# A second staging buffer for q, a shared one for w_spatial, v's key chunks even before odd, and a new step order in a fused attention and gMLP kernel

## Chip, cores, metric

One core of one Trainium2 chip. The metric is the device time of one execution in microseconds; lower is better. Engines are called TensorE (PE in the profile; PEld is its weight load), VectorE (DVE), ScalarE (ACT), GpSimd (POOL) and SyncE (SP, which issues most DMA loads).

## The reference

Grouped-query attention feeds a gMLP block, 8 batches of 384 rows:

```python
scores = q @ k.T / sqrt(64)            # 16 q heads, 4 kv heads, head_dim 64
attn   = softmax(scores)
x      = (attn @ v) as (8, 384, 1024)  # heads side by side
h      = relu(x @ w_in)                # 1024 x 1024
u, v   = h[..., :512], h[..., 512:]
v_n    = (v - mean(v)) / sqrt(var(v) + 1e-6)
v_s    = w_spatial @ v_n + b_spatial   # over the 384 rows
out    = (u * v_s) @ w_out             # 512 x 1024
```

## The kernel before

All work is a hand-ordered list of steps: one text (FIRST) starts batches 0 to 2, one (STEADY) is run for batches 3 to 6, one (LAST) ends. A step is a letter code with its batch: S a pair of score matmuls, E their exp, X the product with v (part 2 gives the row sums), V the v half of x @ w_in, G a pair of half-array groups, lq/lk/lws loads, cq/ck/cws casts to fp16, Tq/Tk/Tw transposes by TensorE, tq/tk/tw the copies of their results, dq/dk transposes by DMA, W a warm-up matmul without use. Each engine takes its own steps in this order and none ahead of it. The last field of a step names an engine: v VectorE, s ScalarE, p GpSimd.

```python
def new_q32(b, gp):                    # fp32 q of one kv pair, one buffer per pair
    loaded["q32", b, gp] = ld.tile(
        [P, 2 * G, NST * D], FP32, name=f"q32_{b}_{gp}", tag=f"q32_{gp}"
    )

def load_w_out(m):
    w32 = stage.tile([P, DM], FP32, name=f"w32_{m}", tag="w32", bufs=2)
    ...

def load_ws():
    ws32 = stage.tile([P, NST, S], FP32, name="ws32", tag="ws32", bufs=1)
    nc.sync.dma_start(ws32, moe_w_spatial.rearrange("(p tt) s -> p tt s", tt=NST))
    loaded["ws32"] = ws32

def score_mm(b, u, j0=0, js=1):
    sc = ps_sc.tile([P, 2, 512], FP32, ..., tag="sc")   # pool ps_sc has two buffers
    ...

def v_mm(b, st, k0=0, k1=NKT):
    ...
    for kc in range(k0, k1):
        nc.tensor.matmul(held["pv", b, st], xT[b][:, kc, ...], w_in16[:, kc, DH:DFF],
                         start=(kc == 0), stop=(kc == NKT - 1))

def norm(b, st):                       # v_n in fp16 from v_r in fp32, both in SBUF
    nc.vector.tensor_scalar(v_n, held["v_r", b, st], mean, rstd,
                            op0=ALU.subtract, op1=ALU.mult)
```

The softmax here doesn't subtract the row's maximum and nothing guards it: scores larger than these inputs give would overflow.

## Time and profile before

| | |
|---|---|
| median of the first 3 runs | 249.28 us (248.23, 249.28, 249.32) |
| the profiled execution | 247.47 us, of which 245.7 from first to last instruction |
| TensorE busy | 97% |

The profile is of one execution. Note for later that this one is 1.8 us faster than the median. The lines of the profile are shown with the prediction. A line of the timeline is: start, duration, engine, source line, operation, out<-in, form, count, and in brackets how long the engine had been idle and what ended that. A line of the waits is: who waited, for whom, total us, times, longest.

### The profile page before, as it was taken

What the parts mean: (1) busy time and instruction counts of PE and PEld (TensorE: products, weight loads), DVE (VectorE), ACT (ScalarE), POOL (GpSimd) and SP (SyncE); (2) the same over time, 40 slices, a digit from 0 to 9 for tenths busy, and PEclk for the clock granted to TensorE, in tenths of its full rate; (3) what the DMA queues carried; (4) which work ended last, traced back from release to release, by engine and by line L of the source; (5) the groups of instructions that cost most, each with busy time, mean ns of one, the idle gap of its engine ahead of it and who ended that gap; (6) DMA issues with size and microseconds to landing.
All of it is one profiled execution on the core that took longest, in us unless ns stands there. A gap on an engine that the chain in (4) does not pass through costs nothing.

```text
span 245.7 us, 6038 instructions
## 1 busy us (share of the span) xinstructions
PE 238.5 (97%) x2556; PEld 114.8 (47%) x2556; DVE 153.1 (62%) x304; ACT 179.7 (73%) x229; POOL 43.9 (18%) x83
## 2 busy tenths in 40 slices
PE   7899999999999999999999999999999999999993
...
ACT  2899999999997778779697787788697797500111
...
GB/s 180 292 211 329 275 256 183 186 309 238 148 210 312 114 235 147 148 60 279 246 223 3 187 296 141 183 30 258 204 197 13 0 173 85 4 69 16 31 230 254
DMA packets 57756, 42.73 MB, mean 174 GB/s; under 512 B 26881, under 2 KB 53889, under 8 KB 57729
## 3 DMA queue, kind: packets, MB, share of 16 engines
...
q10 hardware_dynamic: 1184, 0.39, 0.6%
...
## 4 chain that ended last, share of the span: by engine, by line
PE 93%; ACT 4%; DMA 1%; issue 0%; DVE 0%; POOL 0%
PE X L395 20%; PE sc L368 13%; PE pu L613 13%; PE po L640 12%; PE pv L600 12%; PE pv L438 5%; PE psp L626 5%; PE po L545 4%; PE pu L510 4%; ACT aT L381 3%; PE psp L484 2%; DMA k<-in_k_dram 1%; PE pq L349 1%; PE sc_u L510 1%; PE po L574 0%
## 5 line engine op out<-in xcount | busy, mean ns | idle before, releaser
L381 ACT ACTIVATE aT<-sc 128x1024 f16<-128x1024 f32 x144 | 139.5, 1023 | 19.7 <-PE sc L368 19.5
L640 PE MATMUL po<-w_out,gT 64*128 64x512 f16 x288 | 66.4, 376 | 0.0
L600 PE MATMUL pv<-w_in,xt 64*128 64x512 f16 x272 | 64.2, 376 | 0.0
L368 PE MATMUL sc<-qT,kT 64*128 64x512 f16 x288 | 49.5, 378 | 1.4 <-ACT aT L381 1.3
L424 DVE TENSOR_TENSOR xt<-X,rec 128x512 f16<-128x512 f32 x48 | 31.7, 684 | 15.8 <-ACT aT L381 6.4
L328 DVE COPY osb<-po 128x512 f32<-128x512 f32 x41 | 28.1, 689 | 14.1 <-PE po L640 8.6
L395 PE MATMUL X<-aT,v 128*32 128x512 f16 x576 | 35.9, 380 | 0.0
L613 PE MATMUL pu<-xt,w_in 64*128 64x384 f16 x384 | 35.2, 323 | 0.0
L640 PEld LDWEIGHTS <-gT 64*128 64x128 f16 x288 | 25.6, 94 | 16.1 <-DVE mark_v L694 3.1
L600 PEld LDWEIGHTS <-xt 64*128 64x128 f16 x272 | 25.1, 94 | 15.8 <-issue 2.5
L328 POOL CAST q<-q 128x768 f16<-128x768 f32 (+2 forms) x27 | 20.6, 775 | 53.3 <-DMA q<-in_q_dram 43.3
L522 DVE SCALAR_TENSOR_TENSOR gT<-pu,v_s 128x384 f16<-128x384 f32 x31 | 16.0, 553 | 18.6 <-PE pu L613 15.9
L368 PEld LDWEIGHTS <-kT 64*128 64x128 f16 x288 | 15.1, 94 | 23.5 <-issue 11.9
L613 PEld LDWEIGHTS <-w_in 64*128 64x128 f16 x384 | 18.4, 94 | 14.9 <-issue 1.7
L496 DVE TENSOR_TENSOR v_s<-psp,bias_b 128x384 f32<-128x384 f32 x32 | 20.4, 687 | 3.8 <-PE psp L626 3.0
L395 PEld LDWEIGHTS <-v 128*32 128x32 f16 x576 | 14.8, 97 | 16.5 <-issue 2.8
L395 PE MATMUL X<-aT,ones 128*32 128x512 f16 x288 | 20.0, 382 | 0.0
L406 ACT ACTIVATE rec<-X 128x512 f32<-128x512 f32 x23 | 13.8, 602 | 8.3 <-PE X L395 8.0
L326 ACT ACTIVATE osb<-po 128x512 f32<-128x512 f32 x6 | 3.6, 598 | 18.6 <-PE po L545 17.6
L459 DVE BATCH_NORM_STATS2 stats<-v_r 128x6 f32<-128x512 f32 x24 | 16.6, 691 | 0.7 <-ACT v_r L451 0.5
L412 ACT ACTIVATE rec<-rec 128x512 f32<-128x512 f32 x23 | 14.5, 630 | 0.6
L470 DVE TENSOR_SCALAR v_n<-v_r,mv,rstd 128x512 f16<-128x512 f32 x24 | 12.3, 539 | 3.9 <-issue 2.7
...
## 6 DMA issues: line engine op xcount, KB each, us to landing
...
```

The costliest lines, as they stand in the source:

```text
L328: engine.tensor_copy(dst, src)
L368: nc.tensor.matmul(sc[:, half, 0 : 512 // js], kT[b][lo:hi, gp, t, :], qT[b, gp][lo:hi, qt, j0::js], start=True, stop=True,)
L381: nc.scalar.activation(aT[b, qt][:, gp, t].rearrange("p h (j q) -> p h j q", j=G)[:, :, j0::js], held["sc", b, u, j0][:, :, 0 : 512 // js] ...
L395: nc.tensor.matmul(dst[32 * g : 32 * (g + 1), :], v16[:, g, t, 32 * part : 32 * (part + 1)] if part < 2 else ones32, a[:, g // 2, t, g % 2 ...
L412: nc.scalar.activation(r, r, AF.Exp, scale=-1.0)
L424: nc.vector.tensor_tensor(xt[:, jj, :, qt * P : (qt + 1) * P], held["X", b, qt, jj].rearrange("p (j q) -> p j q", j=G), held["rec", b, qt] ...
L459: nc.vector.bn_stats(s6, held["v_r", b, st])
L496: nc.vector.tensor_tensor(held["v_s", b][:, m, :].rearrange("p (t s) -> p t s", t=NST), held["psp", b, m][:, 0:S].rearrange("p (t s) -> p ...
L522: nc.vector.scalar_tensor_tensor(held["gT", b][:, mu, :], held["pu", b, mu][:, 0:S], 0.0, held["v_s", b][:, mu, :], op0=ALU.max, op1=ALU.mult,
L600: yield lambda kc=kc: nc.tensor.matmul(held["pv", b, st], xT[b][rows, kc, st * P : (st + 1) * P], w_in16[rows, kc, DH:DFF], start=(first a ...
L613: yield lambda kc=kc: nc.tensor.matmul(held["pu", b, mu][:, 0:S], w_in16[rows, kc, mu * P : (mu + 1) * P], xT[b][rows, kc, :], start=(firs ...
L640: yield lambda m=m: nc.tensor.matmul(held["po", b, i], held["gT", b][rows, m, tt * P : (tt + 1) * P], w_out16[rows, m, half * 512 : (half ...
```

## The change

The intent is to let loads go out earlier and to shorten the start: q of the first kv pair gets a second buffer, paid for by staging w_spatial in w_out's buffers and its fp16 cast in an output buffer; v is contracted with the even key chunks first, as these need only one of the two multiplies that make x; and the steps are put in another order, with some casts and evictions on other engines.

```diff
-            [P, 2 * G, NST * D], FP32, name=f"q32_{b}_{gp}", tag=f"q32_{gp}"
+            [P, 2 * G, NST * D], FP32, name=f"q32_{b}_{gp}", tag=f"q32_{gp}", bufs=2 - gp
...
-        w32 = stage.tile([P, DM], FP32, name=f"w32_{m}", tag="w32", bufs=2)
+        w32 = stage.tile([P, NST * S], FP32, name=f"w32_{m}", tag="w32", bufs=2)[:, :DM]
...
-        ws32 = stage.tile([P, NST, S], FP32, name="ws32", tag="ws32", bufs=1)
+        w32 = stage.tile([P, NST * S], FP32, name="w32_s", tag="w32", bufs=2)
+        ws32 = w32.rearrange("p (t s) -> p t s", t=NST)
...
-            loaded["ws16"] = stage.tile([P, NST, NST, P], FP16, name="ws16", tag="ws16", bufs=1)
+            osb = out_pool.tile([P, DM], FP32, name="osb_ws16", tag="osb")
+            loaded["ws16"] = osb.bitcast(FP16)[:, : NST * S].rearrange(
+                "p (s t q) -> p s t q", s=NST, t=NST
+            )
...
+    KC_ORDER = [*range(0, NKT, 2), *range(1, NKT, 2)]
...
-        for kc in range(k0, k1):
+        for n in range(k0, k1):
+            kc = KC_ORDER[n]
```

The three step lists are new throughout. Cut to the steps named, other steps between them left out:

```diff
 FIRST
-(22 warm-ups) Tk,0,0,0,3 W,0,4 W,0,4 tk,0,0,0,3,v cq,0,0,0,1,1,0,1,v Tq,0,0,0,0,1
+(27 warm-ups) Tk,0,0,0,3 W,0,4 cq,0,0,0,1,1,0,1,v Tq,0,0,0,0,1 ... tk,0,0,0,3,s
-lk,2 lws,0 lq,2,0 lbi,0
+lws,0 lk,2 lq,2,0 lbi,0
-S X,0,2,2 V,0,1,4,8 Tq S S X,0,2,0 X,0,2,1 S
+S X,0,2,2 X,0,2,1 X,0,2,0 S S Tq V,0,1,4,8 Tq S
-ck,2,1,0,3,p cq,1,1,1,3,0,0,1,p cws,0,0 ... cws,0,2 cws,0,1 ck,2,0,0,3,p
+cws,0,0 ... cws,0,1 ... cws,0,2 ... ck,2,1,0,3,v ... ck,2,0,0,3,s
 STEADY
-rl,0,0 re,0,0 E E ru,-1,2,s           (ScalarE's order at the start of a period)
+rl,0,0 E cq,1,1,0,3,1,0,1,s re,0,0 ck,1,0,0,3,s E oc,-2,2,s oc,-2,3,s
```

More of the change, by code (lines that the diff above doesn't have):

```diff
@@ L21 @@
 FIRST = """
-W,0,1 W,0,4 lk,0,0,2 lq,0,0,0,1,0,1,s lq,0,1,0,1 W,0,4 W,0,2 W,0,2 W,0,2 W,0,3 W,0,4 lk,0,2,4
-cq,0,0,0,1,0,0,1,s lq,0,0,1,3 lq,0,1,1,3 lk,1 lv,0 lv,1 lq,1,0 lq,1,1 ck,0,0,0,3,p Tk,0,0,0,3 W,0,4
-W,0,4 tk,0,0,0,3,v cq,0,0,0,1,1,0,1,v Tq,0,0,0,0,1 tq,0,0,0,0,1,v W,0,4 ck,0,1,0,3,p
-cq,0,1,0,1,1,0,1,p cq,0,1,0,1,0,0,1,p S,0 lk,2 E,0 lws,0 S,0 Tk,0,1,0,3 W,0,4 W,0,2 lq,2,0 lbi,0
-Tq,0,1,0,0,1 S,0 lwi,0,1,1 lwi,0,1,2 lwi,0,1,3 cq,0,0,1,3,0,0,1,p tq,0,1,0,0,1,v tk,0,1,0,3,v
-cq,0,1,1,3,1,0,1,p cq,0,0,1,3,1,0,1,v W,0,2 E,0 W,0,1 S,0 lq,2,1 E,0 S,0 Tq,0,0,1,0,1 W,0,1 W,0,2
@@ L28 @@
-S,0 cq,0,1,1,3,0,0,1,v tq,0,0,1,0,1,v Tq,0,1,1,0,1 S,0 W,0,4 ck,1,1,0,3,p ck,1,0,0,3,p lwi,0,1,0
-cv,0,p S,0 W,0,1 Tq,0,1,2,0,1 Tk,1,0,0,3 tk,1,0,0,3,v tq,0,1,1,0,1,v tq,0,1,2,0,1,v Tq,0,0,2,0,1
-tq,0,0,2,0,1,v E,0 E,0 E,0 E,0 E,0 S,0 X,0,0,2 S,0 S,0 X,0,0,0 E,0 S,0 rv,0,0 X,0,0,1 xm,0,0,0 E,0
-E,0 S,0 E,0 X,0,1,2 E,0 S,0 xm,0,0,1 X,0,1,1 X,0,1,0 S,0 rl,0,1 E,0 re,0,1 cq,1,0,0,1,0,0,1,p E,0
-S,0 Tk,1,1,0,3 V,0,0,0,4 V,0,0,4,8 lwi,0,0,3 S,0 S,0 cq,1,1,1,3,1,0,1,p lwi,0,0,0 lwi,0,0,2 cv,1,v
-xm,0,1,1 xm,0,1,0 E,0 ck,2,1,0,3,p cq,1,1,1,3,0,0,1,p cws,0,0 lwi,0,0,1 cq,1,0,1,3,1,0,1,v cws,0,2
@@ L34 @@
-cws,0,1 ck,2,0,0,3,p cq,1,0,0,1,1,0,1,s tk,1,1,0,3,v E,0 Tq,1,0,0,0,1 V,0,1,0,4 tq,1,0,0,0,1,v
-ru,0,0,v cq,1,0,1,3,0,0,1,v cq,1,1,0,1,0,0,1,v E,0 cq,1,1,0,1,1,0,1,v S,0 X,0,2,2 V,0,1,4,8
-Tq,1,1,0,0,1 ru,0,1,v S,0 tq,1,1,0,0,1,v E,0 rl,0,2 S,0 X,0,2,0 re,0,2 E,0 E,0 X,0,2,1 xm,0,2,0
-xm,0,2,1 S,0 E,0 Tq,1,0,1,0,1 Tq,1,1,1,0,1 V,0,2,0,4 S,0 S,0 cq,2,0,0,3,1,0,1,p cq,2,0,0,3,0,0,1,p
-cq,2,1,0,3,1,0,1,p cq,2,1,0,3,0,0,1,p E,0 E,0 Tw,0,0,2 bs,0,0 tq,1,0,1,0,1,v bs,0,1 tw,0,0,2
-tq,1,1,1,0,1,v Tq,1,0,2,0,1 V,0,2,4,8 X,1,0,2 S,0 S,0 ru,0,2,s X,1,0,0 rl,1,0 tq,1,0,2,0,1,v bs,0,2
@@ L40 @@
-X,1,0,1 lwo,0,1 dk,2 dq,2,0 lwo,0,0 Tw,0,2,3 Tq,1,1,2,0,1 re,1,0 xm,1,0,0 xm,1,0,1 S,0 E,0 rs,0
-V,1,0,0,4 E,0 tq,1,1,2,0,1,v E,0 nm,0,0 V,1,0,4,8 dq,2,1 tw,0,2,3 nm,0,1 S,0 lwo,0,3 nm,0,2 ru,1,0,v
-G,0,gs,2,0,0,1 S,0 lwo,0,2 mk,0,gs,2,v G,0,gs,0,0,0,1 G,0,gs,2,1,0,1 S,0 mk,0,gs,0,v E,0 E,0 E,0
-sa,0,2 G,0,gs,0,1,0,1 S,0 sa,0,1 sa,0,0 sa,0,3 bs,1,0 X,1,1,2 E,0 cwo,0,1,1,p rl,1,1 X,1,1,0 X,1,1,1
-S,0 cwo,0,0,0,p G,0,gu,2,0,0 S,0 re,1,1 xm,1,1,1 xm,1,1,0 G,0,gu,2,0,1 S,0 cwo,0,0,1,p G,0,gu,0,0,0
@@ L45 @@
-E,0 S,0 G,0,gu,0,0,1 mk,0,gu,2,v G,0,gu,2,1,0 lv,2 cwo,0,1,0,v S,0 lq,3,1 lk,3 lq,3,0 mk,0,gu,0,v
-E,0 E,0 E,0 G,0,gu,2,1,1 S,0 G,0,gu,0,1,0 S,0 G,0,gu,0,1,1 E,0 S,0 cwo,0,3,1,p cwo,0,2,0,p gt,0,2
-gt,0,0 gt,0,1 gt,0,3 cwo,0,3,0,v E,0 cwo,0,2,1,v X,1,2,2 X,1,2,1 S,0 S,0 E,0 E,0 rl,1,2 V,1,1,0,4
-re,1,2 E,0 E,0 V,1,1,4,8 S,0 G,0,go,0,0,0 G,0,go,0,0,1 S,0 xm,1,2,1 ru,1,1,v cv,2,p mk,0,go,0,p
-X,1,2,0 bs,1,1 xm,1,2,0 E,0 E,0 S,0 G,0,go,0,1,0 S,0 G,0,go,0,1,1 X,2,0,2 X,2,0,0 S,0 E,0 E,0
-oc,0,0,v oc,0,1,s rl,2,0 E,0 G,1,w12,2,0,0 re,2,0 G,1,w12,2,0,1 ck,3,0,0,3,s S,0 cq,3,1,0,3,1,0,1,p
@@ L51 @@
-cq,3,1,0,3,0,0,1,p cq,3,0,0,3,1,0,1,p S,0 cq,3,0,0,3,0,0,1,p mk,1,w12,2,v ck,3,1,0,3,v xm,2,0,0 E,0
-G,1,w12,2,1,0 G,1,w12,2,1,1 E,0 ru,1,2,s S,0 E,0 dk,3 lk,4 dq,3,0 lv,3 dq,3,1 oc,0,3,v oc,0,2,v S,0
-X,2,1,2 rl,2,1 re,2,1 bs,1,2 X,2,0,1 X,2,1,1 E,0 X,2,1,0 S,0 xm,2,0,1 xm,2,1,1 G,2,w24,0,0,0
-G,2,w24,0,0,1 S,0 S,0 rs,1 E,0 xm,2,1,0 mk,2,w24,0,v nm,1,0 nm,1,2 nm,1,1 G,2,w24,0,1,0 oc,0,4,v
-G,2,w24,0,1,1 E,0 oc,0,5,v E,0 ru,2,0,s S,0 G,1,gs,0,0,0,1 E,0 S,0 mk,1,gs,0,v G,1,gs,0,1,0,1
-G,1,gs,2,0,0,1 sa,1,0 mk,1,gs,2,v sa,1,1 S,0 G,1,gs,2,1,0,1 S,0 G,1,gu,0,0,0 sa,1,2 sa,1,3 E,0
@@ L57 @@
-G,1,gu,0,0,1 mk,1,gu,0,v S,0 G,1,gu,2,0,0 S,0 G,1,gu,2,0,1 G,1,gu,0,1,0 mk,1,gu,2,v S,0 G,1,gu,2,1,0
-G,1,gu,0,1,1 S,0 G,1,gu,2,1,1 E,0 E,0 gt,1,0 gt,1,1 gt,1,2 gt,1,3 E,0 S,0 X,2,2,2 E,0 X,2,2,0 E,0
-E,0 rl,2,2 E,0 re,2,2 G,2,w10,1,0,0 G,2,w10,1,0,1 S,0 S,0 mk,2,w10,1,v xm,2,2,0 G,2,w10,1,1,0
-oc,1,0,v G,2,w10,1,1,1 S,0 X,2,2,1 oc,1,1,v E,0 E,0 lv,4 st,0,2 lq,4,0 st,0,0 ru,2,1,s cv,3,p bs,2,0
-xm,2,2,1 E,0 lq,4,1 st,1,0 bs,2,1 st,0,1
+W,0,4 W,0,4 W,0,2 lk,0,0,2 W,0,4 W,0,2 W,0,4 W,0,4 W,0,1 W,0,1 lq,0,0,0,1,0,1,s W,0,1 lq,0,1,0,1
@@ new lines @@
+lk,0,2,4 lq,0,0,1,3 lq,0,1,1,3 lk,1 ck,0,0,0,3,p Tk,0,0,0,3 W,0,4 cq,0,0,0,1,0,0,1,s lv,0 lv,1
+lq,1,0 lq,1,1 ck,0,1,0,3,p cq,0,0,0,1,1,0,1,v Tq,0,0,0,0,1 lws,0 lk,2 lq,2,0 lbi,0
+cq,0,1,0,1,1,0,1,p cq,0,1,0,1,0,0,1,p tq,0,0,0,0,1,v W,0,4 tk,0,0,0,3,s S,0 E,0 S,0 Tk,0,1,0,3 S,0
+Tq,0,1,0,0,1 W,0,2 tk,0,1,0,3,v lwi,0,1,1 W,0,2 tq,0,1,0,0,1,v lq,2,1 lwi,0,1,2 cq,0,0,1,3,1,0,1,p
+lwi,0,1,0 lwi,0,1,3 cq,0,0,1,3,0,0,1,v ck,1,0,0,3,p cq,0,1,1,3,0,0,1,v E,0 W,0,1 S,0 S,0
+Tq,0,0,1,0,1 Tq,0,0,2,0,1 E,0 tq,0,0,1,0,1,v cq,0,1,1,3,1,0,1,v tq,0,0,2,0,1,v E,0 W,0,4 S,0 W,0,3
@@ new lines @@
+S,0 Tq,0,1,1,0,1 S,0 W,0,2 Tq,0,1,2,0,1 Tk,1,0,0,3 W,0,2 E,0 cv,0,p E,0 E,0 tq,0,1,2,0,1,v
+tk,1,0,0,3,v tq,0,1,1,0,1,v S,0 X,0,0,2 rv,0,0 S,0 S,0 E,0 X,0,0,0 E,0 S,0 X,0,0,1 E,0
+cq,1,0,0,1,0,0,1,p S,0 E,0 E,0 xm,0,0,0 ck,1,1,0,3,v xm,0,0,1 X,0,1,2 E,0 S,0 X,0,1,0 X,0,1,1 rl,0,1
+E,0 S,0 S,0 V,0,0,0,4 Tk,1,1,0,3 re,0,1 V,0,0,4,8 xm,0,1,1 xm,0,1,0 E,0 E,0 S,0 cq,1,0,0,1,1,0,1,v
+S,0 Tq,1,0,0,0,1 ru,0,0,v tq,1,0,0,0,1,v cq,1,1,0,1,0,0,1,v bs,0,0 tk,1,1,0,3,s E,0 E,0 V,0,1,0,4
+S,0 X,0,2,2 X,0,2,1 X,0,2,0 lwi,0,0,3 lwi,0,0,0 cq,1,1,1,3,0,0,1,p cq,1,1,0,1,1,0,1,p
@@ new lines @@
+cq,1,0,1,3,1,0,1,p cws,0,0 lwi,0,0,1 cws,0,1 cq,1,1,1,3,1,0,1,p cws,0,2 lwi,0,0,2 cv,1,p E,0 rl,0,2
+cq,1,0,1,3,0,0,1,s S,0 S,0 re,0,2 Tq,1,1,0,0,1 E,0 xm,0,2,0 tq,1,1,0,0,1,v V,0,1,4,8
+cq,2,0,0,3,1,0,1,p cq,2,0,0,3,0,0,1,p E,0 xm,0,2,1 ru,0,1,v Tq,1,0,2,0,1 S,0 Tq,1,0,1,0,1 E,0
+cq,2,1,0,3,0,0,1,p cq,2,1,0,3,1,0,1,p tq,1,0,2,0,1,v tq,1,0,1,0,1,v bs,0,1 ck,2,1,0,3,v V,0,2,0,4
+S,0 S,0 E,0 Tq,1,1,1,0,1 Tw,0,0,2 V,0,2,4,8 E,0 X,1,0,2 tw,0,0,2 ru,0,2,v X,1,0,1 tq,1,1,1,0,1,v
+rl,1,0 re,1,0 X,1,0,0 S,0 S,0 bs,0,2 Tw,0,2,3 Tq,1,1,2,0,1 xm,1,0,0 V,1,0,0,4 S,0 rs,0 xm,1,0,1 E,0
@@ new lines @@
+nm,0,2 tw,0,2,3 nm,0,0 nm,0,1 ck,2,0,0,3,s E,0 lwo,0,1 tq,1,1,2,0,1,v E,0 dk,2 dq,2,0 lwo,0,0 dq,2,1
+V,1,0,4,8 lwo,0,3 S,0 lwo,0,2 ru,1,0,v G,0,gs,2,0,0,1 S,0 mk,0,gs,2,v G,0,gs,0,0,0,1 G,0,gs,2,1,0,1
+S,0 mk,0,gs,0,v sa,0,2 E,0 E,0 G,0,gs,0,1,0,1 E,0 S,0 sa,0,3 sa,0,0 X,1,1,2 E,0 rl,1,1 X,1,1,1
+X,1,1,0 S,0 sa,0,1 G,0,gu,2,0,0 S,0 G,0,gu,2,0,1 re,1,1 S,0 xm,1,1,1 xm,1,1,0 G,0,gu,0,0,0 E,0
+mk,0,gu,2,p S,0 cwo,0,1,0,p G,0,gu,2,1,0 G,0,gu,0,0,1 S,0 E,0 S,0 G,0,gu,2,1,1 cwo,0,1,1,v
+mk,0,gu,0,p lv,2 E,0 E,0 G,0,gu,0,1,0 S,0 G,0,gu,0,1,1 lq,3,0 lq,3,1 lk,3 cwo,0,0,1,p cwo,0,3,1,p
@@ new lines @@
+cwo,0,3,0,p S,0 cwo,0,2,1,p cwo,0,0,0,v gt,0,2 gt,0,1 gt,0,3 gt,0,0 bs,1,0 E,0 X,1,2,2 X,1,2,1
+cwo,0,2,0,v E,0 E,0 S,0 E,0 rl,1,2 S,0 V,1,1,0,4 V,1,1,4,8 S,0 G,0,go,0,0,0 S,0 G,0,go,0,0,1
+mk,0,go,0,p E,0 re,1,2 E,0 xm,1,2,1 ru,1,1,s E,0 cv,2,p bs,1,1 E,0 X,1,2,0 X,2,0,2 S,0 G,0,go,0,1,0
+rl,2,0 G,0,go,0,1,1 xm,1,2,0 oc,0,0,v oc,0,1,v S,0 X,2,0,0 S,0 G,1,w12,2,0,0 G,1,w12,2,0,1 S,0 S,0
+E,0 re,2,0 E,0 E,0 mk,1,w12,2,v xm,2,0,0 G,1,w12,2,1,0 cq,3,1,0,3,1,0,1,v G,1,w12,2,1,1
+cq,3,0,0,3,1,0,1,p cq,3,0,0,3,0,0,1,p cq,3,1,0,3,0,0,1,s ck,3,0,0,3,p oc,0,3,v ck,3,1,0,3,p S,0
@@ new lines @@
+ru,1,2,v dq,3,1 E,0 E,0 X,2,1,2 bs,1,2 dk,3 dq,3,0 st,0,0 X,2,0,1 oc,0,2,s E,0 rl,2,1 re,2,1 X,2,1,1
+X,2,1,0 xm,2,0,1 rs,1 xm,2,1,1 S,0 S,0 E,0 nm,1,2 G,2,w24,0,0,0 G,2,w24,0,0,1 nm,1,1 S,0
+mk,2,w24,0,v xm,2,1,0 nm,1,0 S,0 E,0 G,2,w24,0,1,0 oc,0,4,v G,2,w24,0,1,1 E,0 E,0 G,1,gs,0,0,0,1 S,0
+oc,0,5,v ru,2,0,s mk,1,gs,0,v G,1,gs,0,1,0,1 E,0 sa,1,0 sa,1,1 G,1,gs,2,0,0,1 S,0 mk,1,gs,2,p S,0
+G,1,gs,2,1,0,1 G,1,gu,0,0,0 S,0 G,1,gu,0,0,1 S,0 mk,1,gu,0,p sa,1,3 sa,1,2 G,1,gu,2,0,0 E,0 S,0
+G,1,gu,2,0,1 G,1,gu,0,1,0 mk,1,gu,2,p G,1,gu,2,1,0 G,1,gu,0,1,1 S,0 E,0 E,0 E,0 gt,1,1 G,1,gu,2,1,1
@@ L62 @@
+S,0 X,2,2,2 gt,1,3 X,2,2,0 S,0 E,0 gt,1,2 gt,1,0 E,0 E,0 rl,2,2 G,2,w10,1,0,0 E,0 re,2,2
+G,2,w10,1,0,1 S,0 S,0 bs,2,0 mk,2,w10,1,v G,2,w10,1,1,0 E,0 G,2,w10,1,1,1 xm,2,2,0 E,0 oc,1,0,s S,0
+X,2,2,1 oc,1,1,v lq,4,1 st,0,1 st,0,2 lk,4 lq,4,0 lv,3 ru,2,1,v E,0 xm,2,2,1 cv,3,p st,1,0 lv,4
+bs,2,1
 """
 STEADY = """
-cq,1,1,0,3,0,0,1,p X,0,0,2 lk,2 ck,1,1,0,3,p cq,1,1,0,3,1,0,1,p ck,1,0,0,3,p X,0,0,0 S,0 rl,0,0
-G,-1,w12,2,0,0 G,-1,w12,2,0,1 mk,-1,w12,2,v cq,1,0,0,3,1,0,1,p S,0 S,0 re,0,0 E,0 G,-1,w12,2,1,0
@@ L67 @@
-G,-1,w12,2,1,1 E,0 xm,0,0,0 cq,1,0,0,3,0,0,1,v oc,-2,2,v S,0 X,0,1,2 dq,1,0 dk,1 lq,2,0 dq,1,1
-ru,-1,2,s rl,0,1 oc,-2,3,v re,0,1 X,0,0,1 X,0,1,0 X,0,1,1 bs,-1,2 xm,0,0,1 xm,0,1,0 rs,-1 E,0
-G,0,w24,0,0,0 G,0,w24,0,0,1 S,0 S,0 xm,0,1,1 nm,-1,1 mk,0,w24,0,v nm,-1,0 nm,-1,2 E,0 G,0,w24,0,1,0
-G,0,w24,0,1,1 oc,-2,4,v S,0 G,-1,gs,0,0,0,1 mk,-1,gs,0,p S,0 E,0 E,0 oc,-2,5,v ru,0,0,s
-G,-1,gs,2,0,0,1 G,-1,gs,0,1,0,1 mk,-1,gs,2,v G,-1,gs,2,1,0,1 S,0 E,0 E,0 sa,-1,0 S,0 X,0,2,2 sa,-1,2
-sa,-1,1 sa,-1,3 rl,0,2 X,0,2,0 re,0,2 X,0,2,1 E,0 xm,0,2,0 xm,0,2,1 G,-1,gu,0,0,0 G,-1,gu,0,0,1
@@ L73 @@
-mk,-1,gu,0,p S,0 G,-1,gu,2,0,0 G,-1,gu,2,0,1 G,-1,gu,0,1,0 S,0 mk,-1,gu,2,p S,0 bs,0,0 G,-1,gu,0,1,1
-gt,-1,0 gt,-1,1 G,-1,gu,2,1,0 G,-1,gu,2,1,1 gt,-1,3 S,0 gt,-1,2 S,0 G,0,w10,1,0,0 G,0,w10,1,0,1 S,0
-mk,0,w10,1,v S,0 G,0,w10,1,1,0 oc,-1,0,v G,0,w10,1,1,1 E,0 E,0 E,0 oc,-1,1,v E,0 E,0 S,0 E,0 E,0
-lv,2 lq,2,1 E,0 ru,0,1,v E,0 bs,0,1 cv,1,p st,-2,1 st,-1,0 st,-2,2
+X,0,0,2 X,0,0,0 rl,0,0 S,0 G,-1,w12,2,0,0 E,0 cq,1,1,0,3,1,0,1,s re,0,0 G,-1,w12,2,0,1 S,0
+cq,1,0,0,3,0,0,1,p cq,1,0,0,3,1,0,1,p ck,1,0,0,3,s E,0 cq,1,1,0,3,0,0,1,p cv,1,p ck,1,1,0,3,p S,0
@@ new lines @@
+dq,1,0 mk,-1,w12,2,v xm,0,0,0 G,-1,w12,2,1,0 G,-1,w12,2,1,1 ru,-1,2,v S,0 oc,-2,2,s oc,-2,3,s dq,1,1
+X,0,1,2 X,0,0,1 X,0,1,0 X,0,1,1 rl,0,1 re,0,1 dk,1 bs,-1,2 xm,0,0,1 xm,0,1,0 E,0 G,0,w24,0,0,0 E,0
+rs,-1 G,0,w24,0,0,1 xm,0,1,1 S,0 mk,0,w24,0,v S,0 nm,-1,0 nm,-1,1 nm,-1,2 G,0,w24,0,1,0
+G,0,w24,0,1,1 oc,-2,4,v oc,-2,5,v S,0 G,-1,gs,0,0,0,1 S,0 E,0 E,0 mk,-1,gs,0,p ru,0,0,s
+G,-1,gs,2,0,0,1 G,-1,gs,0,1,0,1 mk,-1,gs,2,p S,0 G,-1,gs,2,1,0,1 E,0 sa,-1,0 S,0 X,0,2,2 sa,-1,2 E,0
+sa,-1,3 sa,-1,1 E,0 rl,0,2 X,0,2,1 X,0,2,0 re,0,2 G,-1,gu,0,0,0 S,0 G,-1,gu,0,0,1 xm,0,2,1 xm,0,2,0
```

40 lines of the change are left out of this document (22 added, 18 removed).

## The prediction

> **What bounds the kernel now.** I read first the busy table and the 40 slices, then the groups, then the waits, and last the timeline of the start and of one period.
>
> ```profile
> PE 238.5 (97%) x2556; PEld 114.8 (47%) x2556; DVE 153.1 (62%) x304; ACT 179.7 (73%) x229; POOL 43.9 (18%) x83
> PE   7899999999999999999999999999999999999993
> ACT  2899999999997778779697787788697797500111
> PE 93%; ACT 4%; DMA 1%; issue 0%; DVE 0%; POOL 0%
> ```
>
> TensorE is busy for 97% of the span and carries 93% of the chain that ended last. Busy does not say that it runs at its best rate, so I compare one period with the array's own rate. The waits of TensorE, all of them in the whole run, are three:
>
> ```profile
> PE warm L705 <- POOL ident masks.py:199: 1.4, 1, 1.4
> PE sc L368 <- ACT aT L381: 1.3, 5, 0.5
> PE pk L334 <- POOL k L328: 0.2, 1, 0.2
> ```
>
> The middle one is the only one in which TensorE waits for another engine's steady work: a score matmul needs one of two PSUM score buffers, and the exp of the score before last frees it.
>
> The timeline of TensorE at the start of a period in the middle of the run:
>
> ```profile
> 142.40 0.83 PE L395 MATMUL X<-aT,ones 128*32 128x512 f16 x12
> 143.06 0.82 PE L395 MATMUL X<-aT,v 128*32 128x512 f16 x12
> 143.81 0.39 PE L368 MATMUL sc<-qT,kT 64*128 64x512 f16 x2
> 144.04 0.38 PE L600 MATMUL pv<-w_in,xt 64*128 64x512 f16 x1
> 144.25 0.38 PE L600 MATMUL pv<-w_in,xt 64*128 64x512 f16 x1
> 145.76 0.59 PE L368 MATMUL sc<-qT,kT 64*128 64x512 f16 x4
> 146.20 0.38 PE L640 MATMUL po<-w_out,gT 64*128 64x512 f16 x1
> 147.92 0.38 PE L368 MATMUL sc<-qT,kT 64*128 64x512 f16 x2
> ```
>
> A 0.38 us matmul starts every 0.215 us (144.04 to 144.25), two half-array ones side by side. The same group of the value product starts at 129.81 and 157.87 in the same timeline, so a period (one batch) is 28.06 us. Its content by the step list: 18 score pairs, 27 quarter-width value rows of four, 24 v and 24 output slots of 0.215 us, 32 u and 12 spatial slots of about 0.162 us (384 columns): 93 x 0.2155 + 44 x 0.1625 = 27.2 us. The 0.86 us that remain are nearly all changes of array shape: the score of 147.92 is followed by the value product 0.31 us later where 0.215 would do, and leaving a value product costs 0.13 to 0.15 in the same way; three such visits a period give 3 x (0.105 + 0.14) = 0.74. So the middle of the run holds about 0.1 us of true waiting a period, and no order of the same steps with the same visits can gain more there.
>
> The start is different. The timeline there:
>
> ```profile
> 4.62 0.42 ACT L326 ACTIVATE q<-q 128x256 f16<-128x256 f32 x1 [2.60 <-DMA q<-in_q_dram]
> 4.64 0.36 DVE L328 COPY kT<-pk 128x384 f16<-128x384 f16 x1 [3.73 <-PE pk L334]
> 4.92 0.28 DVE L328 CAST q<-q 128x256 f16<-128x256 f32 x1
> 5.35 0.58 PE L349 MATMUL pq<-ident,q 128*128 128x128 f16 x4
> 5.97 0.42 DVE L328 COPY qT<-pq 128x512 f16<-128x512 f16 x1 [0.77 <-PE pq L349]
> 6.45 0.63 PE L368 MATMUL sc<-qT,kT 64*128 64x512 f16 x4
> 6.90 12.04 ACT L381 ACTIVATE aT<-sc 128x1024 f16<-128x1024 f32 x13 [1.86 <-PE sc L368]
> ```
>
> From 6.90 us ScalarE runs 13 exps without a gap, 0.926 us each, until 18.9. TensorE has no other useful work before about 16 us, so the start is bound by when the first exp begins, and everything after it moves with it.
>
> **What the Trainium skill says.** "TensorEngine Tiling (Array Packing)", section Tiling Modes, states that a change of tiling mode drains the TensorE. The trace agrees: 0.10 to 0.15 us at each change, as worked out above. "TensorE: Matmul & The Clock Gate", Part 1, states that a cold array starts 128-column matmuls every 107 ns and a warm one every 56. The trace agrees in the start: the 8 warm-up matmuls between the k and q transposes took 0.85 us on the chain, 107 ns each. "SBUF — State Buffer", section Who interferes with whom, says that VectorE casts can lock a port pair shared with GpSimd and that PE and ACT wait on nobody. No line here shows the lock; it bears on the change because casts move between these engines.
>
> **The change part by part.** The number of TensorE instructions does not change (5114 rows with the weight loads in both builds), the warm-ups keep their count, and no arithmetic is added. What can move is switches, waits, and the first exp.
>
> First exp. Before, VectorE copies kT (4.64 to 5.00) ahead of its half of the q cast (4.92 to 5.20), and the q transpose waits for that until 5.35. After, kT goes to ScalarE behind its own cast, so the VectorE cast can start at 4.62 when the data is there and end at 4.90; the ScalarE cast (ends 5.04) is then last, and the transpose can start near 5.12. Five more warm-ups stand ahead of the k transpose: 27 x 0.107 + 1.37 = 4.26, 0.15 us later than now (4.10), but four fewer stand behind it, and 4.26 + 7 x 0.107 = 5.01 is still ahead of 5.12. kT on ScalarE: 5.04 + 0.4 = 5.45, ahead of qT. Gain: 5.35 - 5.12, so -0.2 to -0.3 us, say -0.25.
>
> Switches. I counted changes of array shape along the step lists. In the loop and in the last part both have the same number (5 and 6). In the first part there are 57 before and 55 after, since one value product (third query tile of batch 0) becomes a single visit. 2 x 0.12 = -0.24 us on the path, as TensorE has no slack there.
>
> V order. Even chunks need only the first of the two multiplies that make x, so a v product may start 0.68 us earlier (mean of that multiply, 684 ns). It is worth something only where TensorE waits for it, and the waits show no such row: 0 directly, though it is what lets the two steps above be merged.
>
> Second q buffer and shared staging. The load queue waited 4.0 us once for VectorE to free q (the third batch's q, issued at 25.3). It no longer has to; that q may go 5 us earlier. But its transposes landed at about 44.7 for scores of about 48 us, so that is hidden: 0. w_spatial sharing w_out's ring and its cast living in an output buffer only find the space.
>
> Engines in the loop. ScalarE gets two 512-wide evictions (0.60 each), a q cast (estimate 0.78 for 768 columns, from 0.42 for 256 and 0.60 for 512) and a k cast (0.51), and loses a relu (0.60): +1.9 us a period. It now has 18 x 0.97 + 3 x 1.23 + 1.2 + 0.5 = 22.9 of 28.06 us, so it rises to 24.8, 88%. That is still under TensorE's 100%, but two of these stand between the first and second exp of the period. From the period shown: score ready about 144.1, exp to 145.1, q cast to 145.9, the exp of the reciprocal to 146.4, k cast to 146.9, second exp to 147.9. The score that needs its buffer stands at 147.92. Its slack of 0.7 us is used up: 0 to 0.15 us of waiting a period, four periods, +0.1 expected in sum. The later exps of the period (three, four) come out 0.2 to 0.7 us before their scores ask, so the wait should not spread.
>
> Tail. After the last output matmuls both have the same last eviction and store: 0.
>
> Sum: -0.25 - 0.24 + 0.1 = -0.4 us, so 248.9 us from 249.28.
>
> **The rivals.** First, ScalarE becomes a second bound in the loop: if the casts on it take longer than I estimate, or its q data is late, every exp slips and TensorE waits at two or three scores a period, 0.3 to 0.5 us each, 4 periods: +3 to +5 us, about 253. For it: 88% load in strict order, and the wait of 1.3 us for exps is already there. Against it: the loads of both q halves stand half a period ahead of their casts.
>
> Second, the start gains more: if ScalarE is fed without gap to 45 us and the whole bubble of the first 16 us shrinks (TensorE had 22 + 8 + 4 warm-ups there, so it is idle by design), gains of 1 to 2 us are possible: 247.5. Against it: exps run gapless already, so only their first start can move.
>
> Third, a DMA takes the place: the transposes that make kT of the next batch now stand third in the queue, behind both of q, and behind a ScalarE cast. Before, they landed 2.5 us before their score. If they come later by more, TensorE stops once a period, about +1 us each, 252. I think they come about as now, since the q casts begin earlier.
>
> **Range and chances.** The three runs before spread over 1.1 us, so a range of 247.2 to 250.4 holds my sum with its noise and half of each rival. Faster by over 2% (under 244.3) would need 5 us, while the whole loss of TensorE outside switches is about 6 us at the start and the tail: 0.03. Slower by over 2% (over 254.3) needs the first rival in full: 0.03. Within 2%: 0.94.
>
> **What would show it.** In the profile of the changed kernel: the first exp starts near 6.65 instead of 6.90; the period between value products stays at 28.06 within 0.15; the wait of scores for exps rises from 1.3 to 1.5 or 2 us; ScalarE's busy time rises by about 8 us and VectorE's falls. Wrong would be a period of over 28.4 us, a wait of scores for DMA transposes, or a stretch from 7 to 60 us that is over 1 us shorter.

## The result and the profile after

| | before | after |
|---|---|---|
| median (runs) | 248.37 us (6) | 247.12 us (6) |
| lowest to highest | 247.87 to 249.32 | 246.71 to 247.37 |
| ratio of after to before | | 0.994 (0.9916 to 0.9964) |
| the profiled execution | 247.47 us | 247.37 us |

The gain is 0.6%, under the 2% line, so the class "within 2%" held; but 247.12 lies below the range of 247.2 to 250.4, and the gain is three times the 0.4 us forecast.

The odd thing is in the last row: the two profiles are 0.1 us apart. The changed kernel's page, its busy times and its chain:

```profile
PE 238.5 (97%) x2556; PEld 119.3 (49%) x2556; DVE 144.5 (59%) x285; ACT 189.5 (77%) x248; POOL 41.1 (17%) x83
...
PE 92%; ACT 4%; DVE 2%; issue 0%; POOL 0%; POOLq 0%; DVEq 0%
```

And its waits of TensorE:

```profile
PE warm L714 <- POOL ident masks.py:199: 1.4, 1, 1.4
PE sc L373 <- ACT aT L386: 0.9, 4, 0.3
PE sc L373 <- DVE qT L333: 0.3, 1, 0.3
PE pk L339 <- POOL k L333: 0.3, 1, 0.3
```

TensorE's busy time is the same to a tenth, and it still carries the chain (92% against 93%); its waits for exps fell from 1.3 to 0.9 us. In both profiles all of these waits lie in the start, before 16 us. ScalarE rose by 9.8 us and VectorE fell by 8.6, as the moved casts and evictions ask. The start, as far as the first exp:

```profile
4.71 0.29 DVE L333 CAST q<-q 128x256 f16<-128x256 f32 x1 [3.79 <-DMA q<-in_q_dram]
5.03 0.47 ACT L331 ACTIVATE kT<-pk 128x384 f16<-128x384 f16 x1
5.18 0.52 PE L354 MATMUL pq<-ident,q 128*128 128x128 f16 x4
6.64 1.02 ACT L386 ACTIVATE aT<-sc 128x1024 f16<-128x1024 f32 x1 [1.14 <-PE sc L373]
```

The q cast now comes before the kT copy, the q transpose starts at 5.18 instead of 5.35, and the first exp at 6.64 instead of 6.90, where the prediction had 6.65.

So these parts of the start moved as predicted. The two profiled executions as wholes differ by only 0.1 us, though, where the forecast was 0.4. Counted from score to score (from 0, a score being one pair of matmuls), the changed one gains 0.24 us up to the first score, 0.39 from the 18th to the 27th and 0.09 behind the last. It loses 0.06 in the loop and 0.56 between the 27th and the 46th. That loss lies at the first spatial matmuls (about 38 to 39 us). They need the norms, and one norm ran beside GpSimd's casts of q and took 1.15 us, where 0.54 is usual:

```profile
34.95 1.60 POOL L333 CAST q<-q 128x768 f16<-128x768 f32 x2 [3.98 <-DMA q<-in_q_dram]
35.68 1.15 DVE L479 TENSOR_SCALAR v_n<-v_r,mv,rstd 128x512 f16<-128x512 f32 x1
```

The list of waits has no row for it: the recorded idle times there are 0.02 and 0.05 us, since the ends of matmuls are modelled. The loss shows when the starts of the same matmuls are compared with first_only's profile (below), which has no such norm.

Each profile stands at one end of its kernel's runs. Before's is faster than all six runs in the table above, which lie 0.4 to 1.9 us over it; after's is the slowest of its six. What the prediction missed, the common case of before, is thus not in the two profiles.

### The profile page after: what moved, and what is told of

The parts are those of the page before. It is cut to its first block, busy times and chain, and to the rows that moved or that the text cites. A ratio compares the mean times of both kernels' runs of the same rounds, so it can differ in the third digit from the quotient of the medians.

```text
span 245.6 us, 6057 instructions
## 1 busy us (share of the span) xinstructions
PE 238.5 (97%) x2556; PEld 119.3 (49%) x2556; DVE 144.5 (59%) x285; ACT 189.5 (77%) x248; POOL 41.1 (17%) x83
## 4 chain that ended last, share of the span: by engine, by line
PE 92%; ACT 4%; DVE 2%; issue 0%; POOL 0%; POOLq 0%; DVEq 0%
PE X L400 20%; PE pu L622 13%; PE sc L373 13%; PE pv L609 12%; PE po L649 12%; PE psp L635 5%; PE pv L447 4%; PE po L554 4%; PE pu L519 4%; ACT aT L386 3%; PE psp L493 2%; PE warm L714 1%; PE pq L354 1%; DVE v_n L479 1%; PE sc_u L519 1%
## 5 line engine op out<-in xcount | busy, mean ns | idle before, releaser
L373 PE MATMUL sc<-qT,kT 64*128 64x512 f16 x288 | 51.1, 379 | 1.4 <-ACT aT L386 0.9
L622 PE MATMUL pu<-xt,w_in 64*128 64x384 f16 x384 | 36.0, 323 | 0.0
L373 PEld LDWEIGHTS <-kT 64*128 64x128 f16 x288 | 16.2, 94 | 24.1 <-issue 12.5
L622 PEld LDWEIGHTS <-w_in 64*128 64x128 f16 x384 | 20.5, 94 | 12.8 <-issue 1.9
L333 DVE COPY osb<-po 128x512 f32<-128x512 f32 x28 | 19.2, 688 | 11.1 <-PE po L649 7.1
L400 PEld LDWEIGHTS <-v 128*32 128x32 f16 x576 | 16.3, 96 | 14.7 <-issue 1.9
L333 POOL CAST q<-q 128x768 f16<-128x768 f32 (+2 forms) x26 | 18.6, 746 | 24.6 <-DMA q<-in_q_dram 22.5
L331 ACT ACTIVATE osb<-po 128x512 f32<-128x512 f32 x19 | 11.0, 601 | 11.2 <-PE po L554 11.1
L705 POOL MEMSET mark_p<- 1x1 f32 x18 | 1.7, 95 | 103.2 <-PE psp L635 63.0
```

Of the source, the lines that this page charges most:

```text
L333: engine.tensor_copy(dst, src)
L373: nc.tensor.matmul(sc[:, half, 0 : 512 // js], kT[b][lo:hi, gp, t, :], qT[b, gp][lo:hi, qt, j0::js], start=True, stop=True,)
L400: nc.tensor.matmul(dst[32 * g : 32 * (g + 1), :], v16[:, g, t, 32 * part : 32 * (part + 1)] if part < 2 else ones32, a[:, g // 2, t, g % 2 ...
L622: yield lambda kc=kc: nc.tensor.matmul(held["pu", b, mu][:, 0:S], w_in16[rows, kc, mu * P : (mu + 1) * P], xT[b][rows, kc, :], start=(firs ...
```

## The experiments

Two theories at the outset. **A**: in most executions the kernel before loses about 1 us in waits that its one profiled execution happened not to have, and the change removes them. **B**: the difference is noise between runs. Within A: the loss sits in the start (A1) or in the loop (A2).

### Which part of the step lists

> The kernel before, unchanged, timed against itself. The profiled executions of before and after have almost the same span (245.7 and 245.6 us), yet the timed runs differ by 1.2 to 1.5 us. Theory A (the kernel before loses about 1 us in most of its executions, in a wait that its one profiled execution missed): ratio 1.000, median near 248.4, and its second profile likely shows a span of 246.3 or more with a wait that the first does not have. Rival B (the difference is noise between runs): ratio of this control differs from 1 by as much as 0.004.

> The changed kernel with the loop and the last part of before: new start, new buffers, new V order. Theory A1 (the loss sits in the start): near 247.1 us, ratio 0.994 to 0.996. Theory A2 (the loss sits in the loop): near 248.1, ratio 0.998 to 1.000, only the 0.3 us of the earlier first exp and of the switches.

> The kernel before with the loop of the changed kernel alone. Theory A1 (start): near 248.4, ratio 0.999 to 1.002, as the loop gives nothing. Theory A2 (loop): near 247.4, ratio 0.995 to 0.997.

> The kernel before with the last part of the changed kernel alone. Both theories: ratio 0.999 to 1.001, as TensorE has no waits there in either profile; if it shows 0.997 or less, the loss is in the last part or its stores.

The edits swap whole lists:

```diff
 aa_before:    (none)
 first_only:   the changed kernel, with STEADY and LAST of before
 steady_only:  the kernel before, with STEADY of after
 last_only:    the kernel before, with LAST of after
```

| kernel (before: 248.72) | median, range | ratio (95%) |
|---|---|---|
| aa_before | 248.49, 247.57 to 248.75 | 0.9989 (0.9961 to 1.0018) |
| first_only | 247.01, 246.79 to 247.16 | 0.9935 (0.9907 to 0.9964) |
| steady_only | 249.03, 248.25 to 249.91 | 1.0017 (0.9987 to 1.0048) |
| last_only | 248.43, 247.75 to 249.40 | 0.9995 (0.9965 to 1.0025) |

The start (with the buffers and the V order) is the whole gain as far as these runs tell, and its runs spread over 0.4 us where those of before spread over 2.3. B is out, and so is A2. Three of these kernels share before's start, so their profiles are three more samples of it. The waits of TensorE in the unchanged kernel's second profile:

```profile
PE sc L368 <- ACT aT L381: 1.0, 4, 0.4
PE psw L284 <- POOL ws L274: 0.6, 1, 0.6
PE pk L334 <- POOL k L328: 0.5, 1, 0.5
```

The middle line did not exist in the first profile: TensorE stands 0.6 us for GpSimd's cast of w_spatial. Around it in the same profile's timeline:

```profile
29.74 0.71 POOL L274 CAST ws<-ws 128x384 f16<-128x384 f32 x1 [1.53 <-DMA ws<-in_moe_w_spatial_dram]
30.95 1.34 POOL L274 CAST ws<-ws 128x384 f16<-128x384 f32 x2
32.35 0.45 PE L284 MATMUL psw<-ident,ws 128*128 128x128 f16 x5 [0.63 <-POOL ws L274]
...
36.62 1.60 POOL L328 CAST q<-q 128x768 f16<-128x768 f32 x2 [3.88 <-DMA q<-in_q_dram]
37.61 0.88 DVE L470 TENSOR_SCALAR v_n<-v_r,mv,rstd 128x512 f16<-128x512 f32 x1
```

Two things are to be seen. The w_spatial load lands so late that GpSimd, ready since 28.2, waits 1.53 us for it, and the transposes of w_spatial wait for GpSimd. And GpSimd's cast of the third batch's first q (it waited 3.88 us for that load) runs beside VectorE's norm, which takes 0.88 us; a norm alone takes 0.54. In before's first, fast profile the same two lines stand clear of each other:

```profile
34.39 1.60 POOL L328 CAST q<-q 128x768 f16<-128x768 f32 x2 [2.71 <-ACT rec L406]
36.55 0.53 DVE L470 TENSOR_SCALAR v_n<-v_r,mv,rstd 128x512 f16<-128x512 f32 x1
```

In the profiles of steady_only and last_only the w_spatial wait is 0.4 and 0.3 us, the q cast starts at 37.5 and 37.4, and two norms together take 1.74 and 1.75 us instead of 0.99. In steady_only's there is also a third wait of this kind, on w_out:

```profile
PE po L640 <- POOL w_out L328: 1.0, 1, 1.0
```

### Taking the waits away from the kernel before

Theory C: w_spatial comes late. Theory D: that q waits for its only buffer, lands late, and its cast collides with the norms. Theory E: the first exp.

> The kernel before with the w_spatial load ahead of the third batch's k load in the load queue (and GpSimd's cast of that k behind those of w_spatial). Theory C (w_spatial arrives and is cast so late that its transposes often wait): the wait of the w_spatial transposes for GpSimd (0.6, 0.4 and 0.3 us in three of four profiles of this start) is gone, the time falls by 0.3 to 0.6 us, ratio 0.9975 to 0.999. Theory D (late q cast, below) alone: ratio 1.000.

```diff
-lk,2 E,0 lws,0 S,0
+lws,0 E,0 lk,2 S,0
-ck,2,1,0,3,p cq,1,1,1,3,0,0,1,p cws,0,0 ... cws,0,1
+cq,1,1,1,3,0,0,1,p cws,0,0 ... cws,0,1 ck,2,1,0,3,p
```

> The kernel before with two buffers for q of the first kv pair, and w_spatial in w_out's staging to make room; no step moves. Theory D (the third batch's first q waits for its only buffer, lands at 36.5 to 37.4 us in three of four profiles, and GpSimd's casts of it then run beside VectorE's norms and stretch them from 0.54 to 0.88 or more): that q is issued near 20.6 instead of 25.5 us, lands by 35, the norms take 0.54 each, the spatial matmuls do not wait; time falls by 0.2 to 0.6 us, ratio 0.9975 to 0.999. Theory C alone, or a rival in which the early load delays w_spatial: ratio 1.000 or above.

The edit is the four staging hunks of the change and no step.

> Both of the two edits. If C and D both hold they add: 0.6 to 1.0 us, ratio 0.996 to 0.9975, near 247.8. If one of them is all, as that one alone.

> The kernel before with the first kT copy on ScalarE instead of VectorE, nothing else. Theory E (first exp): it starts 0.2 to 0.3 us earlier than the 6.8 to 7.3 us of the four profiles of before, ratio 0.9985 to 0.9995. Rival: the copy is then last on ScalarE and nothing moves: 1.000.

```diff
-tk,0,0,0,3,v
+tk,0,0,0,3,s
```

| kernel (before: 248.28) | median, range | ratio (95%) |
|---|---|---|
| ws_early | 247.72, 247.03 to 249.04 | 0.9988 (0.9963 to 1.0013) |
| q_second_share | 247.38, 246.91 to 247.48 | 0.9965 (0.9948 to 0.9982) |
| both_parts | 247.58, 247.30 to 248.08 | 0.9974 (0.9957 to 0.9992) |
| kt_scalar | 248.63, 247.37 to 249.82 | 1.0016 (0.9988 to 1.0043) |

The buffer with its staging is alone worth 0.9 us of median, more than D asked for, and these runs lie within 0.6 us. (In the repetition below, one run of seven took 249.15.) C and D do not add. Why, the profile of q_second_share shows: it has neither of the two waits. q is issued at 21.0 and lands at 33.2 (before: 25.3 to 25.7, and 34.3 to 37.4 in the four profiles above). But w_spatial, whose place in the queue did not move, also lands earlier: 27.2, against 28.6, 29.7, 29.2 and 29.2. The queues of DMA between 26 and 28 us (packets, MB, share of 16 engines), first aa_before, then q_second_share:

```profile
q0 software_dynamic: 217, 0.21, 74.3%
q1 hardware_dynamic: 108, 0.17, 39.4%
```

```profile
q1 hardware_dynamic: 565, 0.45, 74.7%
q0 software_dynamic: 125, 0.13, 37.5%
```

q1 carries SyncE's loads, w_spatial and q among them, q0 GpSimd's loads of w_in. With q's load already issued, q1 moved 0.45 MB in this stretch instead of 0.17, and the w_in queue less. That q's early issue is what sped w_spatial up is a reading of this correlation (it recurs in q2_merged, 27.5, and q_second_share_2, 27.7). after_q_single below, which takes away the second buffer alone, fits it in one profile; how the DMA engines choose between the queues was not tested. ws_early removed the w_spatial wait from its profile but kept q's late load (34.9), and its runs still reach 249.0. kt_scalar shows nothing over the noise of before, although its profile has the first exp at 6.58: by the 18th score, at 24.88 us, that lead is gone (24.56 to 24.99 in the four profiles of before's start).

Where the buffer's gain lies can be read from the scores. These are means over the four profiles of before's start, and over three with the buffers and before's load order (q_second_share and, from below, q_second_share_2 and q2_warm27):

| us | one buffer | two buffers |
|---|---|---|
| up to the 18th score | 24.80 | 24.89 |
| 18th to 27th (w_spatial's transposes) | 13.90 | 13.49 |
| 27th to 46th (norms, w_out) | 23.40 | 22.89 |

The start up to 24.8 us gains nothing; the two stretches in which the waits stand gain 0.9 us together, as much as the timed runs. The profiles are few, so the division is rough.

### Taking parts from the kernel after

> The changed kernel, unchanged, as the control for the next ones: 247.0 to 247.2 us, ratio 0.994 to 0.996, all runs within 0.7 us.

> The changed kernel with one buffer for q of the first kv pair, all instruction orders the same on every engine. Theory D (the second buffer is the main part): the third batch's q is issued near 25 us again, w_spatial lands 1.5 us later, time near 247.8 to 248.3, ratio 0.998 to 1.000, and the runs spread over 1 us or more. Rival (the new order alone would do, the buffer only lets other things be): 247.2, as the control.

> The changed kernel with the key chunks of v in natural order (one multiply of x is declared earlier so that the order is still safe; no engine's order changes). No TensorE wait for x is in any trace: same as the control within 0.2 us. If the even chunks first matter: 0.2 to 0.7 us slower.

> The kernel before with GpSimd's two casts of the third batch's first q on VectorE, behind the three norms. Theory F (GpSimd's casts of fp32 q stretch VectorE's norms while they overlap): the norms take 0.54 us each in the profile, the spatial matmuls wait for none, time 0.2 to 0.4 us below the kernel before, ratio 0.9985 to 0.9995; the wait for w_spatial stays. Rival (the norms stretch for another reason): durations of 0.88 or more still stand in the profile.

```diff
 after_q_single (on after)
-tag=f"q32_{gp}", bufs=2 - gp
+tag=f"q32_{gp}"
 after_v_natural (on after; and xm,1,0,1 stands ahead of V,1,0,0,4)
-KC_ORDER = [*range(0, NKT, 2), *range(1, NKT, 2)]
+KC_ORDER = [*range(NKT)]
 q_on_vector (on before; dk,2 dq,2,0 lwo,0,0 dq,2,1 follow the casts)
-cq,2,0,0,3,1,0,1,p cq,2,0,0,3,0,0,1,p
+nm,0,2 ru,1,0,v cq,2,0,0,3,1,0,1,v cq,2,0,0,3,0,0,1,v
```

| kernel (before: 248.66) | median, range | ratio (95%) |
|---|---|---|
| after_again | 247.22, 246.97 to 247.40 (and one of 1377.78) | 0.9937 (0.991 to 0.9963) |
| after_q_single | 247.65, 246.92 to 249.94 | 0.9967 (0.993 to 1.0004) |
| after_v_natural | 247.50, 247.08 to 247.66 | 0.9946 (0.9922 to 0.997) |
| q_on_vector | 248.72, 248.41 to 249.05 | 1.0002 (0.9975 to 1.0028) |

Without the second buffer the changed kernel spreads over 3 us again (1.1 without its slowest run) and its median rises by 0.4; the ranges and intervals overlap, so what the buffer does apart from the shared staging is likely, but not shown. That this is less than the 0.9 which the buffer gave to before may come from the changed order, which issues w_spatial ahead of the k load. In the profile, w_spatial landed at 27.3 us instead of 25.7 to 26.3, and TensorE did not wait for it. That profile is of the slowest run (249.94); it lost 2.8 us between the 27th and 46th score, mostly at a DMA transpose of q (1.0), at the gating on VectorE (0.7) and at the casts of w_out (0.9). The V order is worth 0.3 us in the medians, and its profile takes 0.4 us more from the 18th to the 27th score, at a wait for x that the changed kernel's does not have; the ranges overlap, so this is not settled.

q_on_vector was a miss as a cure, and says something on the norms. They took 0.54 and 0.99 (two), as expected, since no GpSimd cast ran beside them; but VectorE then sat in the q casts while TensorE wanted its mark (a small write on VectorE, put there only to hold TensorE's next group back until it). The wait, and then the norm's line of the timeline:

```profile
PE psp L626 <- DVE mark_v L694: 1.0, 1, 1.0
```

```profile
36.29 0.54 DVE L470 TENSOR_SCALAR v_n<-v_r,mv,rstd 128x512 f16<-128x512 f32 x1
```

One wait was traded for another of 1.0 us. On the norms, "SBUF — State Buffer", section Who interferes with whom, says that a VectorE tensor_scalar in a two-port mode and a GpSimd instruction take a shared port pair in turn, and that the later one is blocked whole. In these profiles batch 0's norms were stretched (0.88 instead of 0.54; a pair 1.74 instead of 0.99) only where a GpSimd q cast overlapped them, and in after_q_single the casts stretched too (1.88 instead of 1.60). The trace agrees with the page: in all ten profiles with a stretched norm of batch 0, each such norm ended 0.28 us after the end of a cast, whenever it had started. That is less than a whole norm (0.54), so a part of it was done before the cast ended. In the other order, the seven casts that began 0.16 to 0.72 us into a norm and went on past its end took 0.88 to 1.11 us instead of 0.83, and each ended 0.68 us after the norm. No run here measured the pair by itself.

The second buffer does not end this collision. In six profiles of the changed start with two buffers, q landed at 33.4 to 34.8 us, but the norms came earlier too (35.5 to 36.1), and in four of them the first norm was stretched (0.59, 0.70, 0.91, 1.15). It cost TensorE 0.56 us in after's, at most 0.1 in after_kt_vector's and nothing in the other two.

One execution of after_again, its profiled one, took 1377.78 us and is left out of the ratio. It is described at the end.

### What the rest of the new start gives

> The kernel before with the two buffers and the shared staging alone, once more, so that it stands beside the next ones on one chip: near 247.4 us, ratio 0.996 to 0.997.

> As the one before, and the value product of batch 0's third query tile in one visit, as the changed kernel has it. Theory G (each visit of another array shape that is saved gives 0.12 us on the path): 0.2 to 0.3 us below q_second_share_2. Rival: the v product behind it comes later, and something it feeds waits: the same or slower.

> The changed kernel with the first kT copy back on VectorE ahead of the q cast. Theory E (first exp earlier): 0.2 to 0.4 us above first_only_2, first exp at 6.9 or later in the profile. Rival: the start of the first exp is set by the clock of TensorE and by landings: no difference.

> The changed start with the loop and the last part of before, once more: near 247.0 us, ratio 0.993 to 0.995, 0.3 to 0.5 us below q_second_share_2, from the rest of the new start order.

```diff
 q2_merged (on q_second_share)
-S X,0,2,2 V,0,1,4,8 Tq,1,1,0,0,1 ... S E rl,0,2 S X,0,2,0 re,0,2 E E X,0,2,1
+S X,0,2,2 X,0,2,0 X,0,2,1 V,0,1,4,8 E rl,0,2 Tq,1,1,0,0,1 ... S S re,0,2 E E
 after_kt_vector (on after)
-cq,0,0,0,1,1,0,1,v Tq,0,0,0,0,1 ... tk,0,0,0,3,s
+tk,0,0,0,3,v cq,0,0,0,1,1,0,1,v Tq,0,0,0,0,1
```

| kernel (before: 248.30) | median, range | ratio (95%) |
|---|---|---|
| q_second_share_2 | 247.41, 247.17 to 249.15 | 0.9966 (0.9948 to 0.9983) |
| q2_merged | 248.41, 248.04 to 248.69 | 1.0006 (0.9989 to 1.0022) |
| after_kt_vector | 247.09, 247.00 to 247.81 | 0.9958 (0.9941 to 0.9975) |
| first_only_2 | 246.98, 246.66 to 247.29 | 0.9952 (0.9935 to 0.9969) |

first_only_2 stands 0.4 us below q_second_share_2: that much the new start gives beside the buffers, by the medians. q2_merged is a failed experiment: my merge put the whole value product (36 matmuls) and the second half of V between two scores, so that the 19th score came 1.3 us later after the 18th than in q_second_share. The three scores behind it then stood together, and a new wait came:

```profile
PE sc L372 <- DVE xt L428: 0.9, 1, 0.9
```

It shows that the merge does not pay in this order; the change has two scores at once behind the merged product, and this difference was not tested by itself. What the switches are worth can instead be read from the stretch itself: from the 18th to the 27th score (counted from 0) TensorE took 13.39 us in every profile of before's order that has no wait there (ws_early, q_second_share, both_parts, q_on_vector), and 13.17 us in the changed order (after, first_only, first_only_2, after_kt_vector). The traces have 15 changes of array shape in this stretch before and 13 after, and the same number in every other. That is 0.22 us for the two changes of the one visit saved.

after_kt_vector stands 0.1 us above first_only_2, its first exp at 6.82 instead of 6.53. The first exp itself varies more than the edit moves it: over ten profiles with before's start order it lay between 6.49 and 7.42, mean 6.99; over five with the changed one between 6.53 and 6.92, mean 6.66.

> The kernel before with the two buffers and shared staging, and five of the warm-ups behind the k transpose moved ahead of it (27 ahead, as the changed kernel has), their number unchanged. Theory H (27 in an unbroken row bring TensorE to its full rate sooner, and so the start is shorter and less spread): the runs spread under 0.6 us, time 0.1 to 0.4 us below the 247.4 of q_second_share, full rate by 5.5 us in the profile. Rival (the rate comes when it comes): 247.4 and a spread as before.

> The changed kernel with 22 warm-ups ahead of the k transpose and the other five behind it, their number unchanged. Theory H: 0.1 to 0.4 us above the 247.0 to 247.2 of the changed kernel, spread of 1 us or more, full rate in the profile at 6 us or later. Rival: as the changed kernel.

```diff
 q2_warm27 (on q_second_share)          after_warm22 (on after)
-(22 warm-ups) Tk W,0,4 W,0,4          -(27 warm-ups) Tk W,0,4
+(27 warm-ups) Tk W,0,3                +(22 warm-ups) Tk W,0,4 W,0,3
```

In after_warm22 the last two of the five go behind the first Tq. Medians: 247.50 (247.39 to 247.85), ratio 0.9973 (0.9951 to 0.9994), and 247.05 (246.70 to 247.26), ratio 0.9950 (0.9926 to 0.9973), before 248.15. The theory falls in both directions: q2_warm27 is no faster than q_second_share, after_warm22 no slower than after, and in both profiles TensorE reached its full rate late (7.3 us). Why the first exp varies stays partly open. That TensorE's rate changes at another time in each execution is seen: in the profiles here the first 128-column matmuls at 56 ns after the slow ones at 107 ns start anywhere from 4.3 to 11.4 us. In q_second_share_2's profile, the latest of all (11.4), the first 18 scores took 18.96 us instead of 18.09.

## Why the prediction was right or wrong

**Where TensorE stands in the loop: right.** From the 46th to the last score both before and q_second_share took 148.34 us, after 148.40, first_only 148.30. The loop has nothing to give. Forecast +0.1 us for the new loop, measured 0.06 to 0.1; steady_only, 0.3 us above before in the medians, is not clear of noise. The period, 28.06 us before, is 28.08 after. Only the mark set for it was wrong: the scores' wait for exps fell from 1.3 to 0.9 us instead of rising. All of it lies before 16 us in both profiles, so it never spoke of the loop, and it was no sign for the first rival either. (Both pages have 2556 matmuls and as many weight loads.)

**First exp: right in size, the cause open.** Forecast -0.25; the profiles gave -0.26, the means -0.33. The copy of kT was to bring it, but kt_scalar, which moves that copy alone, is no faster, and after_kt_vector, which moves it back, is only 0.1 us slower. **Switches: right.** Forecast -0.24, measured -0.22. **V order: 0 direct forecast,** 0.3 to 0.4 found, unsettled.

**The step that failed: "Second q buffer and shared staging ... that is hidden: 0."** It was worth 0.9 us alone, in two sets of runs, and 0.7 in a third (q2_warm27). The working looked only at whether q's DMA transposes land before their scores. It did not ask what the late q does on its way there: its casts on GpSimd run beside VectorE's norms and stretch them, and its late issue goes along with a later w_spatial, for which TensorE waits. That the buffers bring the 0.9 us is shown; how it divides between these two ways is argued from few profiles. The line "4.0 us once for VectorE to free q" was the right wait, followed to the wrong end.

**The reading behind it: one profile taken as typical.** The fast execution had almost none of these waits (0.17 us at w_spatial's transposes), so the prediction concluded that there were none to win. Yet the table had the warning: 247.47 us for the profiled execution, 249.28 for the median. Steps worked out from that profile belong to its time: 247.47 - 0.26 - 0.22 + 0.06 = 247.05, and the median of the changed kernel is 247.12. That these agree so closely is in part luck, as its own profiled run took 247.37 with 0.56 us lost at the norms. The 0.9 us between 248.37 and 247.47 are of the size of what the buffers alone gave.

The prediction's own sign of being wrong, "a stretch from 7 to 60 us that is over 1 us shorter", was hidden in the same way. From the first to the 46th score, after took 54.59 us and before's first profile 54.44; the three later profiles of before's start took 55.45, 56.88 and 55.52.

**Rivals.** ScalarE as a second bound: did not come, its exps kept ahead. A late DMA transpose: not in after; it showed once, in after_q_single's slowest run (0.9 us). The second rival, a gain of 1 to 2 us in the start, came nearest, but not by feeding ScalarE without a gap: by taking out waits on loads. Against it I had set that "exps run gapless already", which is true up to 18.9 us and says nothing of what lies behind the 18th score (24.8 us on), where the larger part of the gain lay.

The loop list of before with the start of after (first_only, 247.01 and 246.98) is as fast as the changed kernel or 0.1 us faster; the difference is under what the runs can tell.

## What to carry to other kernels

Compare the profiled execution's time with the median before reading waits from it: if it is faster, the waits that matter are missing from it, and a second profile of the same kernel costs one run. If a profile is the slowest of its runs, its own loss has to be looked for too, and the list of waits may not have it. A load that lands "in time" for its consumer may still place a cast on an engine at a bad moment, so follow a late load through everything it triggers. A buffer that lets a load out early can pay by making slow runs rarer: of 19 runs with the buffers and before's load order, one took more than 247.9 us (249.15); of before's 23 runs beside them, 18 did.

## What the Trainium skill lacked or had wrong

- "TensorEngine Tiling (Array Packing)", Tiling Modes: names the drain at a change of mode, without a cost. Here it is 0.10 to 0.15 us at each change, and the order that saves two of them (15 to 13 in one stretch) takes 0.22 us less.
- "DMA: Bandwidth & Descriptors", Queues, rings and completion order: has no figure for what a longer queue does to the landing of a load in it. Here q1 moved 0.45 MB instead of 0.17 in 2 us when q's load had been issued behind w_spatial, and w_spatial took 7.4 to 7.5 us from issue to landing in four profiles with before's load order, against 8.1 to 9.1 in six without the second buffer. With the changed order it took 9.6 to 10.0 us in six profiles, and 11.0 in the one without the buffer. How the one brings the other was not tested.
- "TensorE: Matmul & The Clock Gate", Part 1: says that the activity window runs freely and the warm-up varies by run, which the start of these profiles shows (4.3 to 11.4 us), and mentions a clock stuck low for over 50 us. Here one execution ran at a low rate for its whole 1376 us: a 512-column matmul every 1.28 us instead of 0.215, with correct results and a granted clock recorded as 1.00. The timeline of it (each row a matmul, half the array):

```profile
511.29 1.62 PE L649 MATMUL po<-w_out,gT 64*128 64x512 f16 x1
512.57 1.62 PE L649 MATMUL po<-w_out,gT 64*128 64x512 f16 x1
513.85 1.79 PE L649 MATMUL po<-w_out,gT 64*128 64x512 f16 x1
```
